# Mirror images and weight forms laid out in denser blocks in HBM

## The chip, the cores and the metric

The kernel runs on one NeuronCore of a Trainium2 chip. The metric is device time in microseconds (us) of one execution of the whole program; three executions of the kernel before took 1409.75, 1408.47 and 1409.6 us, with a median of 1409.6 us. Engines are called by the names that the profile uses: PE is TensorE (matmuls), DVE is VectorE, ACT is ScalarE, POOL is GpSimd, SP is SyncE, which here only issues DMAs.

## The reference

An attention with squared ReLU in place of softmax is followed by two MLPs without residuals, all in float32:

```python
def _attn_ref(u, v, z):            # u, v: 2 x 3008 x 256, z: 2 x 3008 x 64
    scores = (1.0 / S) * np.matmul(z, z.transpose(0, 2, 1))
    attn = np.maximum(scores, 0.0) ** 2
    return u * np.matmul(attn, v)

def reference(...):                # x: 6016 x 256, w_in: 256 x 2048, w_out: 2048 x 256
    x = _attn_ref(u, v, z).reshape(B * S, D)
    r = np.maximum(x @ moe_w_in, 0.0)
    x = (s * (r * r) + b) @ moe_w_out
    h = x @ moe2_w_in
    return (h * (1.0 / (1.0 + np.exp(-1.702 * h)))) @ moe2_w_out
```

The scores are symmetric: z serves as query and as key.

## The kernel before, in words

**Tiling.** The 3008 tokens of each batch are cut into chunks of 512 and a last one of 448 (NCH = 6). Attention goes chunk by chunk of queries (c); for each it runs over the keys in blocks of 128 (kc is the key chunk, t the block of 128 in it). Each float32 operand is split into a rounded part hi, which ACT makes by a cast, and a rest lo, which DVE makes by a subtraction, and the product of a block with v takes six matmuls (L484, L485, L489: v's hi and lo with hi, v's hi with lo), into two accumulators in PSUM, accA and accB by turns.

**Fresh and mirrored blocks.** Because of the symmetry a block of scores between two different chunks is computed once (class Fresh: matmuls L545, ReLU L549, square L552, cast hi L556, lo L560). DVE also transposes it, four blocks of 128 into one wide tile T (L585, 128 x 2048), and `park` writes T to an HBM tile H on GpSimd's DMA queue (L600), 1 MB. When the mirror image is wanted, with the chunks in the other roles, `fetch` reads it back as a wide tile R by four DMAs of 32 partitions each on SP's queue (L613), one for each quarter (x) of the image, and class Turned casts hi (L635) and takes lo (L639) from it. In names the order is bb, kc, c: the blocks with keys of chunk 4 and queries of chunk 2 of batch 0 are gathered in T_0_4_2, parked as H_0_4_2, and fetched as R_0_4_2 when chunk 4 holds the queries and chunk 2 the keys. There are 30 images in the whole run.

**Weights.** During attention the two layers' weights are loaded (wr, L670 and L674), converted on the engines, summed into the forms that the layers' products want, and written to HBM on GpSimd's queue: up_forms (L785, L789), down_whole (L794, quarters of the down weights) and down_forms (L800, L806, five arrays: a11 and s1 to s4). The layers read them again for every pair of chunks: `load_up` (L815, into a wide tile), `load_down` (L828, into a cell) and `load_forms`, which loads one or two of the eight blocks i of one form into one cell: two neighbours in one joined DMA (L842), others by one DMA each (L845).

**Layers.** Chunks go in pairs, in the order PAIRS = (4, 0, 1, 2, 3, 5). A product of 2 x 2 blocks is done with seven products in place of eight for the blocks i that SEVEN lists: all but i = 3 in layer 0 (`0, 1, 2, 4, 5, 6` of 0 to 7, so 3 and 7 are left out), and 0 to 6 in layer 1. Up-projection matmuls are L1088, down-projection ones L1256 and L1281.

**What sets the order.** Nothing is scheduled at run time. The program writes a list of operations, each with what it reads and writes, the engine, and a reckoned cost, and `ordered` lays them out in time for all engines at once; each engine then executes its instructions in that fixed order, each queue its DMAs. A move of kb KB is reckoned by `moves` as a time on a shared DMA pipe (`slow` is the factor that the diff changes):

```python
pipe = 1.05 * slow * kb * 1024 / run * (0.0085 + run / 27200) / 16
```

Tiles come from pools with fixed numbers of buffers (56 cells, 13 big, 5 wide, 4 PSUM tiles, 2 each of accA and accB), and an operation that needs a new tile is held back in the list while no buffer is free. R, T and the up weights share the five wide tiles. Other loads on SP's queue in the attention stage are ur (u, L909, four DMAs into a big tile; DVE transposes it at L927), vr (v, L444), zr (z, L366), and the rows f of the layers (L896).

Of the kernel before, what the change touches and what calls it, by code (L numbers as in the profile page):

```python
# [7 lines left out]
F32 = mybir.dt.float32  # L8
# [220 lines left out]
def attention_mlp_mlp_kernel(  # L229
# [13 lines left out]
    nc = tc.nc  # L243
# [3 lines left out]
    P = 128  # L247
    CH = 512
# [11 lines left out]
    NQ = NF // 2  # L260
# [9 lines left out]
    wide = ctx.enter_context(tc.tile_pool(name="wide", bufs=COUNTS["wide"]))  # L270
    const = ctx.enter_context(tc.tile_pool(name="const", bufs=1))
    hbm = ctx.enter_context(tc.tile_pool(name="hbm", bufs=1, space=bass.MemoryType.DRAM))
# [34 lines left out]
    ops, T = [], {}  # L307
# [10 lines left out]
    STORES = "POOL"  # L318
    to_hbm = dict(SP=nc.sync, POOL=nc.gpsimd)[STORES]

    def moves(kb, fs, reads=(), writes=(), new=(), engine="SP", run=2048, count=None, slow=1.0, **more):
        def f():
            for g in fs:
                g()

        count = count or len(fs)
        pipe = 1.05 * slow * kb * 1024 / run * (0.0085 + run / 27200) / 16
        put(engine, (0.7 if engine == "POOL" else 0.45) * count, 2.0, f, reads, writes, new, pipe=pipe, count=count, **more)

    def move(kb, f, *args, **more):  # L330
        moves(kb, [f], *args, **more)
# [263 lines left out]
    def park(bb, kc, c):  # L595
        key, H = ("T", bb, kc, c), ("H", bb, kc, c)

        def f():
            T[H] = hbm.tile([P, 4 * CH], F32, tag=f"H_{bb}_{kc}_{c}", name=f"H_{bb}_{kc}_{c}")
            to_hbm.dma_start(out=T[H], in_=T[key].rearrange("p b s r -> p (b s r)"))  # L600

        move(1024, f, [key], [H], engine=STORES, soon=0.5)

    def fetch(bb, kc, c):
        H, key = ("H", bb, kc, c), ("R", bb, kc, c)
        fs = []
        for x in range(4):

            def f(x=x):
                if key not in T:  # L610
                    T[key] = wide_tile(f"R_{bb}_{kc}_{c}").rearrange("p (g q) -> p g q", g=4)
                src = T[H].rearrange("(g p) (b q) -> b p g q", g=4, b=4)[x]
                nc.sync.dma_start(out=T[key][32 * x : 32 * x + 32], in_=src)  # L613

            fs.append(f)
        moves(1024, fs, [H], [key], [(key, "wide")], slow=1.55)

    class Turned:
        def __init__(self, session, bb, t, kc, c):
# [26 lines left out]


    up_forms = {(l, i): hbm.tile([P, 14 * P], F32, tag=f"uf{l}{i}", name=f"uf{l}{i}") for l in range(2) for i in range(NQ)}
    down_whole = {(l, i): hbm.tile([P, 2, CH], F32, tag=f"dw{l}{i}", name=f"dw{l}{i}") for l in range(2) for i in range(NQ)}
    down_forms = {  # L650
        (l, f): hbm.tile([P, NQ, 2 * P], F32, tag=f"df{l}{f}", name=f"df{l}{f}")
        for l in range(2)
        for f in ("a11", "s1", "s2", "s3", "s4")
    }
# [73 lines left out]
    def prepare(layer, i, with_sums):  # L728
# [49 lines left out]
            move(kb, lambda: f(T[key].bitcast(F32)), [key], [write], engine=STORES, **more)  # L778

        def part(f):  # L780
            return down_forms[layer, f][:, i].rearrange("p (h n) -> p h n", h=2)

        ws = sums_of(0, *[lambda o=o, k=k: up(o, k) for o in range(2) for k in range(2)])
        key = split(0, [(slice(0, CH), lambda: T[ws])], [ws])
# [7 lines left out]
        key = split(2, [(slice(0, CH), lambda: T[wf][:, :, 2 * P :])], [wf])  # L792
        for o in range(1 if i in always[layer] else 2):
            store(256, key, ("dw", layer, i, o), lambda to, o=o: to_hbm.dma_start(  # L794
                out=down_whole[layer, i][:, o].rearrange("p (h n) -> p h n", h=2),
                in_=to[:, :, 2 * P * o : 2 * P * o + 2 * P],
            ))
        if not with_sums:
# [24 lines left out]
    def load_down(layer, p, i, o):  # L823
        key = "down", layer, p, i, o

        def f():
            t = cell(f"d_{layer}_{p}_{i}_{o}", F32R)
            nc.sync.dma_start(out=t.bitcast(F32), in_=down_whole[layer, i][:, o])  # L828
            T[key] = t.rearrange("p (h n) -> p h n", h=2)

        move(256, f, [("dw", layer, i, o)], [key], [(key, "cell")])
# [2 lines left out]

    def load_forms(layer, p, f, some):
        key = "down", layer, p, f, some
        joined = len(some) == 2 and some[1] == some[0] + 1

        def run():
            t = cell(f"d_{layer}_{p}_{f}_{some[0]}", F32R).rearrange("p (q n) -> p q n", q=2)  # L840
            if joined:
                nc.sync.dma_start(out=t.bitcast(F32), in_=down_forms[layer, f][:, some[0] : some[0] + 2])  # L842
            for y, i in enumerate(some):
                if not joined:
                    nc.sync.dma_start(out=t[:, y].bitcast(F32), in_=down_forms[layer, f][:, i])  # L845
                T[key, i] = t[:, y].rearrange("p (h n) -> p h n", h=2)

        count = 1 if joined else len(some)
        moves(
            128 * len(some), [run], [("df", layer, f, i) for i in some], [key], [(key, "cell")], run=1024, count=count  # L850
        )
        for i in some:
            form_key[layer, p, i, f] = key
# [650 lines left out]
    def write_list():  # L1504
# [59 lines left out]
        for layer in range(2):  # L1564
            for p in PAIRS:
# [10 lines left out]
                for i, quad in enumerate(pair.quads):  # L1576
# [4 lines left out]
                        load_forms(layer, p, "s4", (i,))  # L1581
                    if some and i == NQ - 1:
                        for f in ("a11", "s1", "s2", "s3"):
                            for x in range(0, len(some), 2):
                                load_forms(layer, p, f, some[x : x + 2])
                        for x, names in enumerate(tail_of(pair)):
                            fixed.setdefault(k + 4 + x, []).extend(names)
                    if (layer, p, i) == (0, PAIRS[0], 4):
# [70 lines left out]
```

## Time and profile before

| | |
|---|---|
| time, median of 3 | 1409.6 us |
| the profiled execution: its time | 1408.94 us |
| its span | 1407.2 us |
| PE busy | 1387.8 us (99%), 6147 matmuls |
| PE weight loads (PEld) busy | 1148.5 us (82%) |
| DVE busy | 1310.3 us (93%), 2324 instructions |
| ACT busy | 1190.0 us (85%), 2308 instructions |
| POOL busy | 148.6 us (11%), 235 instructions |
| DMA | 322.61 MB, 229 GB/s in the mean |
| mean granted clock of PE | 0.997 |

The span runs from the first to the last recorded instruction; the execution takes 1.7 us more. Busy shares are means over the whole run, and weight loads run beside matmuls. Attention fills about the first 440 us, the layers the rest. In the rows shown further down, a releaser in brackets, as in [4.19 <-DMA R<-H], says that the engine sat idle for 4.19 us before this instruction and that a DMA into R from H ended the wait; SPq is the DMA queue that SyncE feeds. In lists of operations several equal ones in a row stand as one row with a count.

### The profile page before, as it was taken

The page shows a single profiled execution, that of the slowest core. Times are in us where ns is not written, and L with a number is a line of the kernel's source. Part 1 is how long each engine was busy: PE and PEld are TensorE (multiplying, and loading weights), DVE is VectorE, ACT ScalarE, POOL GpSimd, SP SyncE. Part 2 cuts the span into 40 slices and gives each one's busy share as a digit, 9 for nine tenths or more (in the row PEclk, how much of TensorE's full clock was granted, in tenths as well). Part 3 has the DMA queues.
Part 4 walks back from the last instruction along what each step waited for, and adds up shares of the span by engine and source line. Part 5 has one row for each costly group of instructions (what it writes and reads, how often), then busy time and mean ns, then how long its engine had stood idle before and what let it go on. Part 6 is the DMA issues. An engine that isn't in the chain of part 4 may idle for free.

```text
span 1407.2 us, 20260 instructions
## 1 busy us (share of the span) xinstructions
PE 1387.8 (99%) x6147; PEld 1148.5 (82%) x6147; DVE 1310.3 (93%) x2324; ACT 1190.0 (85%) x2308; POOL 148.6 (11%) x235
## 2 busy tenths in 40 slices
PE   8999999999999999999999999999999999999998
PEld 5888779888888888787888888888888788888897
DVE  7999886999998699999999999999989999999987
ACT  8999675999877598998989899998878796978685
POOL 3022210002211000001010101100010101010010
PEclk9999999999999999999999999999999999999999
DMA  7899898869999556677768576866757575666553
GB/s 171 245 296 282 250 276 197 239 211 269 274 246 342 187 198 210 254 239 266 258 214 270 200 260 215 291 222 212 252 175 268 160 267 161 230 199 198 181 183 105
DMA packets 194829, 322.61 MB, mean 229 GB/s; under 512 B 85408, under 2 KB 117728, under 8 KB 190880
## 3 DMA queue, kind: packets, MB, share of 16 engines
q1 hardware_dynamic: 172976, 241.69, 57.4%
q0 software_dynamic: 19008, 78.90, 15.6%
q10 hardware_dynamic: 2736, 0.74, 0.3%
q8 instruction: 48, 0.79, 0.2%
q14 instruction: 61, 0.50, 0.1%
HBM read 244.19 MB, written 77.07 MB: 228 GB/s over the span
## 4 chain that ended last, share of the span: by engine, by line
PE 81%; issue 6%; DVE 4%; DMA 3%; ACT 3%; SPq 2%; ACTq 0%; POOL 0%; DVEq 0%; POOLq 0%
PE ps_b L1088 8%; PE ps_d L1088 8%; PE ps_c L1088 8%; PE accB L1281 6%; PE ps_s L545 5%; PE accA L485 4%; PE accA L484 4%; PE ps_d L1281 4%; PE accA L489 4%; PE ps_a L1088 4%; PE accB L484 4%; PE accB L485 4%; PE accB L489 4%; PE ps_b L1281 4%; PE accA L1281 3%
## 5 line engine op out<-in xcount | busy, mean ns | idle before, releaser
L1211 DVE TENSOR_TENSOR lo<-g_c,hi 128x512 fp32r<-128x512 f32 (+1 forms) x540 | 345.3, 672 | 6.4 <-ACT hi L1207 5.4
L1207 ACT CAST hi<-g_c 128x512 fp32r<-128x512 f32 (+1 forms) x540 | 310.9, 616 | 9.7 <-DVE g_c L1196 6.8
L1088 PE MATMUL ps_d<-op_t,up 128*128 128x512 f32 (+1 forms) x432 | 121.6, 390 | 2.0 <-DVE g_c L1162 1.7
L1088 PE MATMUL ps_b<-op_t,up 128*128 128x512 f32 (+1 forms) x432 | 121.3, 389 | 1.0 <-ACT s_u L1137 0.9
L549 ACT ACTIVATE a<-ps_s 128x512 f32<-128x512 f32 (+1 forms) x168 | 103.2, 621 | 21.4 <-PE ps_s L545 21.4
L484 PE MATMUL accA<-hi,v 128*128 128x512 f32 x288 | 112.7, 391 | 2.0 <-ACT hi L556 2.0
L1174 ACT ACTIVATE g_c<-g_c 128x512 f32<-128x512 f32 (+1 forms) x144 | 89.5, 622 | 29.2 <-DVE g_c L1162 28.7
L485 PE MATMUL accA<-hi,v 128*128 128x512 f32 x288 | 113.0, 392 | 0.0
L560 DVE TENSOR_TENSOR lo<-a,hi 128x512 fp32r<-128x512 f32 (+1 forms) x156 | 103.8, 668 | 9.7 <-ACT hi L556 8.6
L552 ACT ACTIVATE a<-a 128x512 f32<-128x512 f32 (+1 forms) x168 | 110.6, 665 | 0.9
L484 PE MATMUL accB<-hi,v 128*128 128x512 f32 (+1 forms) x288 | 110.0, 382 | 0.8 <-DVE hi L566 0.8
L485 PE MATMUL accB<-hi,v 128*128 128x512 f32 (+1 forms) x288 | 109.8, 381 | 0.0
L556 ACT CAST hi<-a 128x512 fp32r<-128x512 f32 (+1 forms) x168 | 108.2, 649 | 0.7
L1196 DVE TENSOR_TENSOR g_c<-g_c,g_c 128x512 f32<-128x512 f32 (+1 forms) x156 | 105.0, 673 | 1.4
L545 PE MATMUL ps_s<-zq,zk 128*128 128x512 f32 (+1 forms) x336 | 101.6, 390 | 2.8 <-DVE zk L394 2.2
L1088 PEld LDWEIGHTS ps_d<-op_t,up 128*128 128x128 f32 x432 | 79.5, 188 | 21.7 <-DVE g_c L1162 5.3
L1088 PEld LDWEIGHTS ps_b<-op_t,up 128*128 128x128 f32 x432 | 79.7, 188 | 19.9 <-DVE g_c L1162 2.8
L1281 PE MATMUL accB<-hi,d 128*128 128x512 f32 (+1 forms) x312 | 95.0, 386 | 0.0
L585 DVE STREAM_TRANSPOSE T<-a 128x512 f32<-128x512 f32 x120 | 83.9, 700 | 7.9 <-DMA H<-T 4.7
L1177 ACT ACTIVATE g_c<-g_c 128x512 f32<-128x512 f32 (+1 forms) x144 | 88.2, 629 | 0.6
L639 DVE TENSOR_TENSOR lo<-R,hi 128x512 fp32r<-128x512 f32 x120 | 79.4, 678 | 7.9 <-ACT hi L635 3.6
L489 PE MATMUL accA<-lo,v 128*128 128x512 f32 x276 | 85.8, 392 | 0.3 <-DVE lo L560 0.3
(181 smaller groups left out, 3418.9 us busy)
## 6 DMA issues: line engine op xcount, KB each, us to landing
up<-uf SPq DMA_DIRECT2D x96, 896.0 KB
H<-T POOLq DMA_DIRECT2D x30, 1024.0 KB, 7.5
R<-H SPq DMA_DIRECT2D x120, 256.0 KB
d<-dw SPq DMA_DIRECT2D x114, 256.0 KB
d_s<-df1s SPq DMA_DIRECT2D x54, 256.0 KB
d_s<-df0s SPq DMA_DIRECT2D x72, 128.0 KB
f<-rows SPq DMA_DIRECT2D x18, 512.0 KB
d_s<-df0s SPq DMA_DIRECT2D x36, 256.0 KB
```

What stands on the lines that cost most here:

```text
L484: nc.tensor.matmul(T[k][:, :n], w[:, 0, cols], T[hi][:, :n], **start_flags(k, fresh))
L485: nc.tensor.matmul(T[k][:, :n], w[:, 1, cols], T[hi][:, :n], **start_flags(k, ()))
L489: nc.tensor.matmul(T[k][:, :n], w[:, 0, cols], T[lo][:, :n], **start_flags(k, ()))
L545: nc.tensor.matmul(T[self.p][:, :n], k, T[zq][:, h, :n], start=h == 0, stop=h == 1)
L552: nc.scalar.activation(out=T[self.a][:, :n], in_=T[self.a][:, :n], func=AF.Square)
L556: nc.scalar.copy(out=T[self.hi][:, :n], in_=T[self.a][:, :n])
L560: nc.vector.tensor_tensor(out=T[self.lo][:, :n], in0=T[self.a][:, :n], in1=T[self.hi][:, :n], op=ALU.subtract)
L1088: nc.tensor.matmul(to[:, :n], a[h], y[:, g, :n], start=first and j == 0, stop=False, skip_group_check=True)
L1196: nc.vector.tensor_tensor(out=self.get(to), in0=self.get(x), in1=self.get(y), op=ALU.subtract)
L1207: nc.scalar.copy(out=T[keys[0]][:, :n], in_=self.get(c))
L1211: nc.vector.tensor_tensor(out=T[keys[1]][:, :n], in0=self.get(c), in1=T[keys[0]][:, :n], op=ALU.subtract)
L1281: nc.tensor.matmul(to[:, :n], w[:, h, cols], g[:, :n], start=first and j == 0, stop=False, skip_group_check=True)
```

## The change

Three things change, and the order that follows from them.

First, an image lies in HBM as four quarters, H being [4, 128, 512] in place of [128, 2048]. The store still writes all four quarters of 128 partitions, now in pieces of 512 floats; a fetch of quarter x reads one contiguous block of 256 KB. The list reckons the store with a factor of 1.1 (1.0 before) and the fetches with 1.2 (1.55 before).

Second, down_whole is [2, 128, 512] in place of [128, 2, 512], and down_forms is [4, 128, 2, 256] in place of [128, 8, 256], two neighbouring blocks in one dense array.

Third, a joined load of two forms is now only possible for an even and the next odd block. In layer 0 the six blocks 0, 1, 2, 4, 5, 6 are therefore grouped as (0, 1), (2, 6), (4, 5), where they were (0, 1), (2, 4), (5, 6).

```diff
     def park(bb, kc, c):
...
-            T[H] = hbm.tile([P, 4 * CH], F32, tag=f"H_{bb}_{kc}_{c}", name=f"H_{bb}_{kc}_{c}")
-            to_hbm.dma_start(out=T[H], in_=T[key].rearrange("p b s r -> p (b s r)"))
-        move(1024, f, [key], [H], engine=STORES, soon=0.5)
+            T[H] = hbm.tile([4, P, CH], F32, tag=f"H_{bb}_{kc}_{c}", name=f"H_{bb}_{kc}_{c}")
+            to_hbm.dma_start(out=T[H].rearrange("b p q -> p b q"), in_=T[key].rearrange("p b s r -> p b (s r)"))
+        move(1024, f, [key], [H], engine=STORES, soon=0.5, slow=1.1)
...
     def fetch(bb, kc, c):
...
-                src = T[H].rearrange("(g p) (b q) -> b p g q", g=4, b=4)[x]
+                src = T[H][x].rearrange("(g p) q -> p g q", g=4)
                 nc.sync.dma_start(out=T[key][32 * x : 32 * x + 32], in_=src)
...
-        moves(1024, fs, [H], [key], [(key, "wide")], slow=1.55)
+        moves(1024, fs, [H], [key], [(key, "wide")], slow=1.2)
...
-    down_whole = {(l, i): hbm.tile([P, 2, CH], F32, tag=f"dw{l}{i}", name=f"dw{l}{i}") for l in range(2) for i in range(NQ)}
+    down_whole = {(l, i): hbm.tile([2, P, CH], F32, tag=f"dw{l}{i}", name=f"dw{l}{i}") for l in range(2) for i in range(NQ)}
...
-        (l, f): hbm.tile([P, NQ, 2 * P], F32, tag=f"df{l}{f}", name=f"df{l}{f}")
+        (l, f): hbm.tile([NQ // 2, P, 2, 2 * P], F32, tag=f"df{l}{f}", name=f"df{l}{f}")
...
-        joined = len(some) == 2 and some[1] == some[0] + 1
+        joined = len(some) == 2 and some[1] == some[0] + 1 and some[0] % 2 == 0
...
-                            for x in range(0, len(some), 2):
-                                load_forms(layer, p, f, some[x : x + 2])
+                            both = [(x, x + 1) for x in range(0, NQ, 2) if x in some and x + 1 in some]
+                            odd = [x for x in some if (x - x % 2, x - x % 2 + 1) not in both]
+                            for group in sorted(both + [tuple(odd[x : x + 2]) for x in range(0, len(odd), 2)]):
+                                load_forms(layer, p, f, group)
```

The accesses to down_whole and down_forms in `prepare`, `load_down` and `load_forms` follow the new shapes.

The order of DMAs on SP's queue, in the attention stage around the fetches of the images R_0_4_2 and R_0_4_3; before:

```order
L670 DMA wr_0_9_2045<-in_moe_w_in_dram 128x1x256 x2
L674 DMA wr_0_9_2045<-in_moe_w_out_dram 128x512
L909 DMA ur_3_2058<-in_u_dram 32x16x64 x4
L613 DMA R_0_4_2_2092<-H_0_4_2_1538 32x4x512 x4
L613 DMA R_0_4_3_2151<-H_0_4_3_1832 32x4x512 x4
L613 DMA R_0_5_0_2200<-H_0_5_0_786 32x4x512 x4
L909 DMA ur_4_2255<-in_u_dram 32x16x64 x4
L444 DMA vr_1_1_2297<-in_v_dram 32x4x256 x4
L613 DMA R_0_5_1_2400<-H_0_5_1_1218 32x4x512 x4
L613 DMA R_0_5_2_2462<-H_0_5_2_1623 32x4x512 x4
L613 DMA R_0_5_3_2515<-H_0_5_3_1982 32x4x512 x4
```

And after the change:

```order
L670 DMA wr_0_9_1989<-in_moe_w_in_dram 128x1x256 x2
L674 DMA wr_0_9_1989<-in_moe_w_out_dram 128x512
L613 DMA R_0_4_2_2051<-H_0_4_2_1548 32x4x512 x4
L613 DMA R_0_4_3_2076<-H_0_4_3_1832 32x4x512 x4
L909 DMA ur_3_2125<-in_u_dram 32x16x64 x4
L909 DMA ur_4_2165<-in_u_dram 32x16x64 x4
L613 DMA R_0_5_0_2202<-H_0_5_0_786 32x4x512 x4
L444 DMA vr_1_1_2267<-in_v_dram 32x4x256 x4
L670 DMA wr_0_10_2292<-in_moe_w_in_dram 128x1x256 x2
L674 DMA wr_0_10_2292<-in_moe_w_out_dram 128x512
L613 DMA R_0_5_1_2324<-H_0_5_1_1247 32x4x512 x4
L444 DMA vr_1_2_2416<-in_v_dram 32x4x256 x4
```

Both fetches move ahead of the load ur_3, ur_4 ahead of R_0_5_0, and the weight load wr_0_10 and the v load vr_1_2 ahead of R_0_5_1 and R_0_5_2.

The order on ScalarE at the first casts of R_0_4_2 (L549, L552 and L556 belong to the chunk's own fresh blocks, L763 to the weights that are prepared on the side); before:

```order
L635 CAST hi_2211<-R_0_4_1_1925 128x512
L549 ACTIVATE a_2214<-ps_s_2195 128x512
L552 ACTIVATE a_2214<-a_2214 128x512
L556 CAST hi_2223<-a_2214 128x512
L635 CAST hi_2234<-R_0_4_2_2092 128x512
L549 ACTIVATE a_2236<-ps_s_2218 128x512
L635 CAST hi_2240<-R_0_4_2_2092 128x512
L552 ACTIVATE a_2236<-a_2236 128x512
L549 ACTIVATE a_2260<-ps_s_2242 128x512
L556 CAST hi_2266<-a_2236 128x512
```

And after the change:

```order
L635 CAST hi_2217<-R_0_4_1_1911 128x512
L549 ACTIVATE a_2219<-ps_s_2207 128x512
L552 ACTIVATE a_2219<-a_2219 128x512
L556 CAST hi_2228<-a_2219 128x512
L635 CAST hi_2239<-R_0_4_2_2051 128x512
L549 ACTIVATE a_2243<-ps_s_2225 128x512
L763 CAST forms_0_4_1_2248<-wf_0_8_2170 128x256
L552 ACTIVATE a_2243<-a_2243 128x512
L763 CAST forms_0_4_2_2261<-wf_0_8_2170 128x512
L556 CAST hi_2272<-a_2243 128x512
L549 ACTIVATE a_2275<-ps_s_2250 128x512
L763 CAST forms_0_4_1_2248<-wf_0_8_2170 128x128
```

The first cast of R_0_4_2 keeps its place between the fresh blocks' operations; its second cast comes later, and the casts of a weight form have moved in before it.

## Rows read from the trace of the kernel before

**Rows 1.** Part 1 of the page: each engine's busy us, share, instructions.
```profile
PE 1387.8 (99%) x6147; PEld 1148.5 (82%) x6147; DVE 1310.3 (93%) x2324; ACT 1190.0 (85%) x2308; POOL 148.6 (11%) x235
```

**Rows 2.** Chain that ended last, 995 to 1010 us: start, us, what.
```profile
995.97 4.08 PE ps_b L1281 x18
```

**Rows 3.** Busy by 20 us: PE, PEld, DVE, ACT, POOL; clock, DMA, GB/s.
```profile
140.00:160.00 20.00, 18.77 (x82) 14.64 (x81) 15.23 (x28) 12.34 (x24) 4.09 (x6) 1.00 0.91 243
...
180.00:200.00 20.00, 17.97 (x72) 14.27 (x72) 16.62 (x36) 12.02 (x24) 3.24 (x5) 0.91 1.10 282
300.00:320.00 20.00, 20.00 (x90) 16.58 (x89) 19.77 (x39) 18.07 (x36) 1.07 (x2) 1.00 0.71 218
560.00:580.00 20.00, 18.71 (x80) 14.34 (x79) 19.67 (x34) 18.88 (x37) 5.26 (x8) 1.00 0.88 314
640.00:660.00 20.00, 18.21 (x78) 14.19 (x77) 18.07 (x31) 17.39 (x34) 3.44 (x5) 1.00 0.87 295
```

**Rows 4.** Chain that ended last, 130 to 200 us.
```profile
172.67 1.94 SPq L613
...
176.19 7.75 DMA R<-H
...
188.60 0.85 PE accA L489 x2
```

**Rows 5.** Timelines of ACT and PE: start, us, work, idle time before it.
```profile
184.03 0.62 ACT L635 CAST hi<-R 128x512 fp32r<-128x512 f32 x1 [4.19 <-DMA R<-H]
...
187.23 0.50 PE L484 MATMUL accA<-hi,v 128*128 128x512 f32 x1 [2.03 <-ACT hi L556]
```

**Rows 6.** Timeline of SP's queue, 100 to 200 us.
```profile
129.35 2.59 SPq L909 DMA_DIRECT2D ur<-in_u_dram  x4
...
160.58 11.99 SPq L909 DMA_DIRECT2D ur<-in_u_dram  x4
```

**Rows 7.** By 1 us from 412: us, granted clock, DMA share, GB/s.
```profile
413.00:414.00 1.00, 1.00 1.02 221
414.00:415.00 1.00, 1.00 1.08 231
```

**Rows 8.** The same by 0.5 us from 1079, and SP's timeline before it.
```profile
1079.00:1079.50 0.50, 1.00 1.11 420
1079.50:1080.00 0.50, 1.00 1.03 395
...
1075.52 1.91 SPq L842 DMA_DIRECT2D d_s<-df1s  x3
```

**Rows 9.** SP's timeline from 176 us, and 1 us of all engines.
```profile
214.69 3.67 SPq L444 DMA_DIRECT2D vr<-in_v_dram  x4
...
220.00:221.00 1.00, 1.00 (x6) 0.93 (x6) 0.68 (x2) 0.55 (x2) 0.00 (x0) 1.00 1.09 225
```

**Rows 10.** Timeline of DVE, 140 to 200 us.
```profile
160.64 0.68 DVE L639 TENSOR_TENSOR lo<-R,hi 128x512 fp32r<-128x512 f32 x1
...
199.34 0.70 DVE L927 STREAM_TRANSPOSE ut<-ur 128x512 f32<-128x512 f32 x1
```

**Rows 11.** DMA issues (count, KB, us to landing), and the image tile's landings.
```profile
out_dram<-o POOLq DMA_DIRECT2D x40, 128.0 KB, 3.0
...
DMA to landing us min/median/max: 4.2/7.5/10.9
```

**Rows 12.** DVE's and POOL's timelines, and SP's waits (us, times, longest).
```profile
152.23 0.71 DVE L585 STREAM_TRANSPOSE T<-a 128x512 f32<-128x512 f32 x1 [4.70 <-DMA H<-T]
...
141.61 0.57 POOL L600 DMA_DIRECT2D H<-T  x1 [4.77 <-DVE T L585]
...
SPq L613 <- DMA H<-T: 91.4, 10, 16.8
```

**Rows 13.** ACT's and PE's timelines at the next chunk.
```profile
221.60 0.57 ACT L556 CAST hi<-a 128x448 fp32r<-128x448 f32 x1
...
216.16 0.36 PE L484 MATMUL accB<-hi,v 128*128 128x448 f32 x1
```

More of the change, by code (lines that the diff above doesn't have):

```diff
@@ L780, in part @@
         def part(f):
-            return down_forms[layer, f][:, i].rearrange("p (h n) -> p h n", h=2)
+            return down_forms[layer, f][i // 2, :, i % 2].rearrange("p (h n) -> p h n", h=2)
         ws = sums_of(0, *[lambda o=o, k=k: up(o, k) for o in range(2) for k in range(2)])
@@ L794, in prepare @@
             store(256, key, ("dw", layer, i, o), lambda to, o=o: to_hbm.dma_start(
-                out=down_whole[layer, i][:, o].rearrange("p (h n) -> p h n", h=2),
+                out=down_whole[layer, i][o].rearrange("p (h n) -> p h n", h=2),
                 in_=to[:, :, 2 * P * o : 2 * P * o + 2 * P],
@@ L827, in f @@
             t = cell(f"d_{layer}_{p}_{i}_{o}", F32R)
-            nc.sync.dma_start(out=t.bitcast(F32), in_=down_whole[layer, i][:, o])
+            nc.sync.dma_start(out=t.bitcast(F32), in_=down_whole[layer, i][o])
             T[key] = t.rearrange("p (h n) -> p h n", h=2)
@@ L841, in run @@
             if joined:
-                nc.sync.dma_start(out=t.bitcast(F32), in_=down_forms[layer, f][:, some[0] : some[0] + 2])
+                nc.sync.dma_start(out=t.bitcast(F32), in_=down_forms[layer, f][some[0] // 2])
             for y, i in enumerate(some):
                 if not joined:
-                    nc.sync.dma_start(out=t[:, y].bitcast(F32), in_=down_forms[layer, f][:, i])
+                    nc.sync.dma_start(out=t[:, y].bitcast(F32), in_=down_forms[layer, f][i // 2, :, i % 2])
                 T[key, i] = t[:, y].rearrange("p (h n) -> p h n", h=2)
```

## The prediction

> **What bounds the kernel now.** I read first the page's busy table, then the busy time by stretches of 20 us, then the chain that ended last around the two worst stretches, and last the timelines of the engines that it names. The table has TensorE busy for 1387.8 us of the 1407.2 us span [rows 1], so everything outside it is 19.4 us. A busy matmul can still be a slow one, so I counted matmuls. Eighteen 512-column matmuls in a row take 4.08 us [rows 2], 226.7 ns each; 20 us hold 88.2 of them. The undisturbed stretch at 300 us shows 90 (those across an edge count in both neighbours), the one at 140 us 82, the one at 180 us 72, at a granted clock of 0.91, and two in the later layers 80 and 78 [rows 3]. In time that is 1.4, 3.7, 1.9 and 2.3 us lost. So TensorE is the bound and only such gaps can be won: about 5 us in the attention stage, the rest in the layers behind it, beside the start and the end, which the change doesn't touch.
>
> The gap at 180 us has its cause in the chain: the next image fetch is issued only at 172.67, it is still in flight at 176.19, for 7.75 us more, and the chain ends in two matmuls that take 0.85 us [rows 4], where two at full speed take 0.45. [...] What stood ahead of that fetch on the SP queue was the line that loads u, L909: its four loads took 11.99 us from 160.58, beside large stores; the same four took 2.59 us at 129 us [rows 6].
>
> **The fetches themselves.** The list now reckons an image fetch 1.2/1.55 = 0.77 times as long as before. Does it get shorter? With almost nothing but image fetches running, the DMA engines are full (a share of 1.02 and 1.08) at 221 to 231 GB/s [rows 7]. One fetch moves 2 KB pieces that lie 8 KB apart in HBM into 32 partitions. The joined weight-form loads of L842 move 2 KB pieces, also 8 KB apart, into 128 partitions: three of them were issued from 1075.52, and adding up the bytes of the queue puts them into the stretch from about 1079.1 to 1081, which ran at 395 to 420 GB/s [rows 8]. The other way round, the v loads of 214.69, whose source is a dense block but whose target is 32 partitions, end the plateau at 220 us, at 225 GB/s [rows 9]. So the rate goes with the partitions written, not with the gaps in the source, and the change leaves the 32 partitions as they are. I take the fetch as unchanged, 1.05 MB at 223 GB/s = 4.7 us for the four pieces of an image; the other end is 400 GB/s, 2.6 us.
>
> [...]
>
> The weight forms (down_whole, down_forms) get denser too. Their loads already run at 395 to 420 GB/s from pieces 8 KB apart, so I cost them at 0. The regrouping in layer 0, (0,1), (2,6), (4,5) for (0,1), (2,4), (5,6), issues the same four DMAs.
>
> **What moves.** Since a fetch is reckoned shorter, the list sets the SP queue anew. The image R_0_4_2, the one that was late, and R_0_4_3 now go ahead of the u load ur_3, not behind it. ur_3 costs nothing there: the transposes that read it began at 199.34 us [rows 10], 27 us after its issue ended. R_0_4_2 needs a free wide tile; R_0_3_1 was read for the last time at 160.64 + 0.68 = 161.3 [rows 10], by counting L639's reads back from those of the late image. So it can be issued at 161.3 instead of 172.67, 11.3 us earlier. Even if it takes as long as before, from 172.67 to 176.19 + 7.75 = 183.9, thus 11.3 us, it lands at 172.6; ScalarE comes to it at 184.03 - 4.19 = 179.8. The wait goes with 7 us to spare, and the lost 3.7 us with it: **-3.7 us**. What is late next there is work of the same engines that ran without waits.
>
> **The stores.** A store now writes 512 pieces of 2 KB instead of 128 of 8 KB; no such store is in the trace. Nearest rows: the output stores, 512 pieces in 128 KB, land after 3.0 us; the image stores after 4.2 at best, 7.5 median [rows 11]. Taking off the data at 400 GB/s (0.3 and 2.6 us) leaves 2.7 against 1.6 us: at most 1.1 us more per store. Who waits: VectorE's transposes at 152.23 waited 4.70 us for the store issued at 141.61, whose landing frees their tile [rows 12], and TensorE lost the 1.4 us of that stretch. A later landing costs there one for one. [...] Between -1.4 and +1.1 I take **+0.6**, nearer to the row of 512 pieces. On GpSimd itself nothing waits but more stores.
>
> **The layers behind.** Of 6165 TensorE instructions some 570 change places, line and buffer numbers set aside, most of them in layer 0 (from the next weights' decoding, the regrouping, and the order of row loads). Losses there are gaps of 1 to 2 us like those at 560 and 640 us, behind ScalarE or VectorE, none behind a DMA. I cost the shuffle at 0, between -3 and +3, the size of one and a half such gaps.
>
> Sum: -3.7 + 0.6 = -3.1 us. The profiled execution took 1408.94 us, 1.7 us above its span; the median of 1409.6 is 0.7 higher, and I carry the difference over: 1409.6 - 3.1 = **1406.5 us**, mostly faster by more than the 0.2% (2.8 us) that a measurement of this kernel can tell from no change.
>
> **Rivals.** First, given back at the next chunk: behind ur_4 the new queue puts the loads wr_0_10 and vr_1_2 ahead of R_0_5_1 and R_0_5_2. At 400 and 223 GB/s they take 1.3 and 2.35 us, so R_0_5_3 could come 3.7 us later. Its casts stand on ScalarE ahead of the chunk's own block, whose cast ended at 222.2; TensorE, which began this chunk at 216.16 [rows 13], needs it 48 matmuls of 448 columns (198 ns) later, at 225.7. Spare is 3.5 us, and TensorE now comes 3.7 us earlier: the gain would go again, 1409.5 to 1410. Against it: the queue has won back about 9 us from the slow u load, so these fetches should come earlier, not later. 20%.
>
> Second, the list is right and the fetches do run at up to 400 GB/s. Then the shortened queue also takes most of the remaining 1.7 us of this stage, and images leave room for the stores: about 1404. Rows 7 to 9 speak against it. 10%.
>
> Third, slower: the 2 KB stores land much later. Place: the tile that the transposes at 152 us wait for, and the fetches that follow a store at once (SP waited for a store's landing ten times, 91.4 us [rows 12]). If landings grow by g, TensorE loses g at 152 us and about g at two fetches without spare; 3g - 3.7 passes +2.8 us from g = 2.2 us on. At g = 3 the time is 1409.6 - 3.7 + 9 = 1415. For it: that one store already took 10.6 us to land. Against: the piece count bounds it at 1.1 us. 14%.
>
> Fourth, layer 0's new order loses two more gaps like that at 640 us and a further one like that at 560: +6.5, with the rest about 1413. 8%.
>
> **How the numbers follow.** The forecast has 48%; its own range, from the bounds (-3.7 - 1.4 - 3 and -3.7 + 1.1 + 3), is 1401.5 to 1410. It gives 40 points of faster and 8 of no change; the second rival adds 10 of faster, the first 16 of no change and 4 of slower, the third 14 of slower, the fourth 3 and 5. That is 50% faster, 27% within 0.2%, 23% slower. For 8 in 10 the range runs from 1401.5 to 1412.5; it leaves out the third rival's far end and part of the fourth.
>
> **What would show it.** In the trace of the changed kernel: plateaus of fetches still near 223 GB/s (at 400 the second rival holds); ScalarE's cast of R_0_4_2 without a wait and the matmul count of that stretch near 88 at a granted clock of 1.00; no new ScalarE wait on R_0_5_3 that ends in a TensorE gap near 225 us; image stores landing at 7.5 to 8.6 us in the median, and the transposes' wait of 4.7 us neither gone nor over 6. The prediction is wrong if R_0_4_2 finds no free tile, if TensorE stalls at the next chunk, or if layer 0 loses more than it did.

## The result and the profile after

The changed kernel takes 1420.26 us in the median of five runs (1419.11 to 1422.71), the kernel before 1409.28 us in five; the ratio is 1.0085, with a 95% interval of 1.007 to 1.010. The forecast was 3 us faster; it is 11 us slower, above the range. The profiled execution took 1420.26 us, its span is 1418.5 us. The page's table, against [rows 1]:

```profile
PE 1393.1 (98%) x6147; PEld 1151.1 (81%) x6147; DVE 1313.0 (93%) x2324; ACT 1189.7 (84%) x2308; POOL 154.3 (11%) x235
```

TensorE is busy for 5.3 us more with the same matmuls, and outside its busy time lie 25.4 us, not 19.4. The busy time by stretches of the changed kernel, to be held against [rows 3]:

```profile
140.00:160.00 20.00, 18.07 (x73) 13.95 (x72) 14.07 (x26) 12.75 (x24) 3.74 (x5) 0.91 0.94 259
180.00:200.00 20.00, 19.86 (x88) 16.10 (x87) 19.94 (x41) 15.20 (x30) 5.31 (x8) 1.00 0.97 278
200.00:220.00 20.00, 15.71 (x57) 12.13 (x56) 12.35 (x22) 9.93 (x20) 1.58 (x3) 0.83 0.99 266
220.00:240.00 20.00, 18.86 (x92) 16.94 (x92) 11.80 (x21) 12.61 (x26) 0.00 (x0) 1.00 0.86 188
480.00:500.00 20.00, 17.62 (x74) 14.63 (x73) 12.21 (x26) 11.47 (x22) 0.67 (x1) 0.91 0.31 109
640.00:660.00 20.00, 20.00 (x88) 16.00 (x87) 19.87 (x36) 15.53 (x29) 1.80 (x3) 1.00 0.54 190
```

The stretch at 180 us has its 88 matmuls, as forecast. But the one at 200 us has 57, at a granted clock of 0.83, and at 480 us, early in layer 0, 74 are left. In the kernel before the same two stretches were full:

```profile
200.00:220.00 20.00, 20.00 (x92) 16.93 (x91) 14.12 (x25) 13.52 (x26) 3.45 (x5) 1.00 1.06 269
480.00:500.00 20.00, 20.00 (x90) 16.62 (x89) 19.29 (x33) 19.08 (x36) 0.68 (x1) 1.00 0.50 184
```

So that stretches of all runs can be compared, here is the time that TensorE loses in each: its length less 226.7 ns for each matmul of 512 columns in it and 198 ns for each of 448, an estimate from the same time per column (from 229.95 us of the kernel before 28 of them in a row took 5.67 us, 202.5 ns each); a matmul across an edge counts in each stretch by its part. Single values are good to about a microsecond, and an undisturbed 200 to 300 us shows 0.7.

| lost, us | 0 to 200 | 200 to 300 | 300 to 470 | 470 to 500 | rest |
|---|---|---|---|---|---|
| before | 15.4 | 0.7 | 1.2 | 0.2 | 25.1 |
| changed | 13.7 | 11.2 | 1.7 | 4.6 | 22.7 |

The layers behind even win 2.4 us and the first 200 us 1.7; the loss, 10.5 and 4.4 us more than before, stands at two places. How the first comes about is seen on SP's queue. Its timeline after the change (start, us, line, what, count), against [rows 9]:

```profile
187.50 1.80 SPq L444 DMA_DIRECT2D vr<-in_v_dram  x4
189.51 1.51 SPq L670 DMA_DIRECT2D wr<-in_moe_w_in_dram  x2
191.81 0.35 SPq L674 DMA_DIRECT2D wr<-in_moe_w_out_dram  x1
192.83 4.80 SPq L613 DMA_DIRECT2D R<-H  x4
197.73 8.85 SPq L444 DMA_DIRECT2D vr<-in_v_dram  x4
207.17 11.16 SPq L613 DMA_DIRECT2D R<-H  x12
```

R_0_5_1 is issued at 192.83, R_0_5_2 only at 207.17 (199.29 in the kernel before); between them stands vr_1_2, which took 8.85 us to issue. The chain that ended last, there and at the matmuls that follow:

```profile
189.51 11.45 DMA wr<-in_moe_w_in_dram
200.96 0.02 issue
200.98 5.39 DMA vr<-in_v_dram
...
207.17 3.93 DMA R<-H
...
214.43 0.85 PE accA L489 x2
```

The weight load wr_0_10 of 189.51 was 11.45 us in flight. A load of vr_1_2 that stands eight places behind it was issued 0.02 us after it had landed. The cast of R_0_5_2 then kept ScalarE waiting, and the operation behind it TensorE, in the timelines of ACT, DVE and PE:

```profile
211.16 0.62 ACT L635 CAST hi<-R 128x512 fp32r<-128x512 f32 x1 [6.36 <-DMA R<-H]
...
206.38 0.43 DVE L685 TENSOR_SCALAR pw<-wr 128x512 uint32<-128x512 uint32 x1 [3.18 <-DMA vr<-in_v_dram]
...
212.35 0.79 PE L484 MATMUL accA<-hi,v 128*128 128x512 f32 x1 [3.22 <-ACT hi L556]
```

While the wr load was in flight the DMA engines were full (a share of 1.04 to 1.06), with an image store and four stores of prepared weights, issued from 189.29 to 193.33, among others. By 2 us (granted clock, DMA share, GB/s):

```profile
188.00:190.00 2.00, 1.00 1.06 235
196.00:198.00 2.00, 1.00 1.04 414
200.00:202.00 2.00, 1.00 1.06 386
```

The second place is a store that lands late. The chain at the start of layer 0, and the matmul behind it in PE's timeline:

```profile
475.65 5.96 DMA df1s<-forms
...
481.75 0.62 ACT op_b L989
...
482.91 0.97 PE L1088 MATMUL ps_a<-op_b,up 128*128 128x512 f32 x3 [2.38 <-ACT ps_a L1154]
```

A store of layer 1's weight forms, 5.96 us from issue to landing, holds up a cast of op_b, an early operand of layer 0, and TensorE waits 2.38 us behind it; in the kernel before GpSimd issued no store between 431 and 482 us.

### The profile page after: what moved, and what is told of

Same layout as the page of the kernel before. It is cut to its first block, busy times and chain, and to the rows that moved or that the text cites. A ratio compares the mean times of both kernels' runs of the same rounds, so it can differ in the third digit from the quotient of the medians.

```text
span 1418.5 us, 20194 instructions
## 1 busy us (share of the span) xinstructions
PE 1393.1 (98%) x6147; PEld 1151.1 (81%) x6147; DVE 1313.0 (93%) x2324; ACT 1189.7 (84%) x2308; POOL 154.3 (11%) x235
## 4 chain that ended last, share of the span: by engine, by line
PE 74%; DVE 8%; DMA 7%; ACT 5%; issue 3%; SPq 1%; POOL 0%; ACTq 0%; DVEq 0%; POOLq 0%
PE ps_b L1088 8%; PE ps_c L1088 8%; PE ps_d L1088 7%; PE accB L1281 7%; PE ps_d L1281 5%; PE ps_b L1281 4%; PE ps_a L1088 4%; PE ps_s L545 4%; PE accA L1281 3%; PE accA L485 3%; PE accA L484 3%; PE accA L489 3%; PE ps_c L1281 3%; PE accA L1256 3%; PE accB L484 3%
## 5 line engine op out<-in xcount | busy, mean ns | idle before, releaser
L1207 ACT CAST hi<-g_c 128x512 fp32r<-128x512 f32 (+1 forms) x540 | 310.0, 616 | 12.1 <-DVE g_c L1196 8.6
L549 ACT ACTIVATE a<-ps_s 128x512 f32<-128x512 f32 (+1 forms) x168 | 102.5, 614 | 19.9 <-PE ps_s L545 19.9
L552 ACT ACTIVATE a<-a 128x512 f32<-128x512 f32 (+1 forms) x168 | 109.9, 658 | 1.0
L556 ACT CAST hi<-a 128x512 fp32r<-128x512 f32 (+1 forms) x168 | 107.5, 642 | 1.7 <-issue 1.1
```

The lines of the kernel that those rows point to most:

```text
L552: nc.scalar.activation(out=T[self.a][:, :n], in_=T[self.a][:, :n], func=AF.Square)
L556: nc.scalar.copy(out=T[self.hi][:, :n], in_=T[self.a][:, :n])
L1207: nc.scalar.copy(out=T[keys[0]][:, :n], in_=self.get(c))
```

## Experiments: list, images or weights

Theory A was that the new order costs the time, because 1.2 tells the list of a fetch that doesn't exist; B, that the 2 KB stores cost it; C, the weight layouts and the regrouping. Three kernels take the parts one by one. e1_list_only is the kernel before with the factors alone:

```diff
-        move(1024, f, [key], [H], engine=STORES, soon=0.5)
+        move(1024, f, [key], [H], engine=STORES, soon=0.5, slow=1.1)
...
-        moves(1024, fs, [H], [key], [(key, "wide")], slow=1.55)
+        moves(1024, fs, [H], [key], [(key, "wide")], slow=1.2)
```

> Only the two factors of the list are changed (fetch 1.2, store 1.1); images, weight forms and grouping stay as before. Theory A, the new order costs the time (the queue is set as if fetches were shorter, which they are not): 1417 to 1421 us, with the TensorE gap of about 5 us at 207 to 217 us and the one of about 4.7 us at 480 us. Theory B, the 2 KB stores cost it: 1408 to 1410 us, or less by the 3 us of the gap at 185 us. Theory C, the regrouping and the weight layouts: the same as B.

1425.31 us, 1.0122 (1.0104 to 1.0139) times the kernel before, above the range of theory A. Every engine's order is that of the changed kernel, and the same two places lose: 14.0 us at 200 to 300, 5.8 at 470 to 500. All of the loss is in the two numbers; it is even 5 us larger than in the changed kernel.

e2_images_only is the kernel before with the new H alone, without the factors:

```diff
-            T[H] = hbm.tile([P, 4 * CH], F32, tag=f"H_{bb}_{kc}_{c}", name=f"H_{bb}_{kc}_{c}")
-            to_hbm.dma_start(out=T[H], in_=T[key].rearrange("p b s r -> p (b s r)"))
+            T[H] = hbm.tile([4, P, CH], F32, tag=f"H_{bb}_{kc}_{c}", name=f"H_{bb}_{kc}_{c}")
+            to_hbm.dma_start(out=T[H].rearrange("b p q -> p b q"), in_=T[key].rearrange("p b s r -> p b (s r)"))
...
-                src = T[H].rearrange("(g p) (b q) -> b p g q", g=4, b=4)[x]
+                src = T[H][x].rearrange("(g p) q -> p g q", g=4)
```

> Only the layout of the image tile in HBM is changed, with the factors of before, so every engine keeps the order of before. Theory A: 1408 to 1411 us, store landings a little longer (8 us in the median), fetch plateaus still at 220 to 230 GB/s. Theory B: 1413 to 1420 us. If the fetches were really quicker from dense quarters: plateaus above 300 GB/s and 1404 to 1407 us.

1407.51 us, 0.9994 (0.9983 to 1.0005). The order is that of before on every engine, the stores land after 8.2 us in the median, and the time is the same: B falls.

e3_weights_only is the changed kernel with these lines and those of e1 as they were before:

```diff
-            T[H] = hbm.tile([4, P, CH], F32, tag=f"H_{bb}_{kc}_{c}", name=f"H_{bb}_{kc}_{c}")
+            T[H] = hbm.tile([P, 4 * CH], F32, tag=f"H_{bb}_{kc}_{c}", name=f"H_{bb}_{kc}_{c}")
...
-        moves(1024, fs, [H], [key], [(key, "wide")], slow=1.2)
+        moves(1024, fs, [H], [key], [(key, "wide")], slow=1.55)
```

> Only the layouts of the weight forms and the regrouping in layer 0 are changed; images and factors as before, so that the attention stage keeps its order. Theory C: the loss of some 11 us stands here. Theories A and B: 1407 to 1411 us, with nothing moved before 440 us.

1408.42 us, 0.9997 (0.9988 to 1.0007): C falls too. e17_layouts_only, run last, has all layouts and the regrouping, and the factors of before:

```diff
-        move(1024, f, [key], [H], engine=STORES, soon=0.5, slow=1.1)
+        move(1024, f, [key], [H], engine=STORES, soon=0.5, slow=1.0)
...
-        moves(1024, fs, [H], [key], [(key, "wide")], slow=1.2)
+        moves(1024, fs, [H], [key], [(key, "wide")], slow=1.55)
```

> The changed kernel with the two factors of before (fetch 1.55, store 1.0): all layouts and the regrouping stay. If layouts and order add up as e2 and e3 did alone: 1406 to 1410 us. If they cost something together: over 1411 us.

1403.80 us, 0.9969 (0.9957 to 0.9981), faster than either expectation. Without the two numbers the change gains 4.6 us. Between e1 and the changed kernel, which have one order, the layouts gave 5 us as well. Why they give more together than e2 and e3 apart isn't settled; e17 has the order of e3 on every engine, so the list plays no part in it; in the profile of e17 the late cast of [rows 5] no longer waits.

## Experiments: what the fetch is bound by

e4_wide_fetch is the kernel before with the four DMAs cut the other way, each into all 128 partitions:

```diff
-                src = T[H].rearrange("(g p) (b q) -> b p g q", g=4, b=4)[x]
-                nc.sync.dma_start(out=T[key][32 * x : 32 * x + 32], in_=src)
+                src = T[H].rearrange("(g p) (b q) -> g b p q", g=4, b=4)[x]
+                nc.sync.dma_start(out=T[key][:, x], in_=src)
```

> Everything as before, order included, but the four DMAs of a fetch are cut the other way: each writes 512 columns of all 128 partitions in place of 2048 columns of 32. Theory of partitions (the fetch rate goes with the partitions written): plateaus of fetches at 380 to 420 GB/s and a time of 1403 to 1408 us. If the gaps in the source or the 2 KB pieces set the rate: plateaus stay at 220 to 230 GB/s and the time within 1408 to 1411 us.

1559.88 us, 1.1075 (1.1058 to 1.1091), neither expectation. With little but fetches running, e4 moves, by 1 us:

```profile
161.00:162.00 1.00, 1.00 0.27 98
163.00:164.00 1.00, 0.50 0.26 102
```

A quarter of the DMA engines' share of before, 0.26 to 0.27 for the 1.02 to 1.08 of [rows 7], and half the rate, 98 to 102 GB/s for 221 to 231. The source's outermost dimension had become 4 (it was 32); that this sets the share was my reading.

e7_rows_fetch keeps the 128 partitions and gives the source 128 rows, by another H; the store becomes four DMAs, the factors are 1.55 and 1.0:

```diff
-            T[H] = hbm.tile([4, P, CH], F32, tag=f"H_{bb}_{kc}_{c}", name=f"H_{bb}_{kc}_{c}")
-            to_hbm.dma_start(out=T[H].rearrange("b p q -> p b q"), in_=T[key].rearrange("p b s r -> p b (s r)"))
+            T[H] = hbm.tile([P, 4 * CH], F32, tag=f"H_{bb}_{kc}_{c}", name=f"H_{bb}_{kc}_{c}")
+            rows_of = T[H].rearrange("(b j) (g q) -> g j b q", b=4, g=4)
+            for g in range(4):
+                to_hbm.dma_start(out=rows_of[g], in_=T[key][32 * g : 32 * g + 32].rearrange("p b s r -> p b (s r)"))
...
-                src = T[H][x].rearrange("(g p) q -> p g q", g=4)
-                nc.sync.dma_start(out=T[key][32 * x : 32 * x + 32], in_=src)
+                src = T[H][:, CH * x : CH * x + CH]
+                nc.sync.dma_start(out=T[key][:, x], in_=src)
```

> The image lies in HBM as the fetch wants it, one 8 KB row for each partition of R; each of the four DMAs of a fetch writes 512 columns of all 128 partitions from 128 rows, and the store is cut into four DMAs of 32 partitions. Factors of before (1.55, 1.0), weights as in the changed kernel. The fourfold outer dimension of e4, which left a quarter of the DMA engines' share in use, is gone. Theory of partitions: plateaus at 380 to 420 GB/s and 1402 to 1408 us, or up to 1411 if the narrower stores land 2 to 3 us later. If 2 KB pieces set the rate: 220 to 230 GB/s.

1401.21 us, 0.9950 (0.9935 to 0.9964), the fastest of all, 2.6 us under e17, though the two intervals overlap. Each quarter of its image stores lands after 5.6 us in the median, and the transposes at 152 us of [rows 12] don't wait. e11_rows_095 has the same fetches reckoned at 0.95:

```diff
-        moves(1024, fs, [H], [key], [(key, "wide")], slow=1.55)
+        moves(1024, fs, [H], [key], [(key, "wide")], slow=0.95)
```

> e7 (fetches into all 128 partitions), now with a fetch reckoned at 0.95, which is 2.7 us in the list and what 1.05 MB take at 400 GB/s. Theory A1 (a price that is true gives a good order): 1397 to 1403 us. Rival: a short price pulls weight loads and stores together whatever the fetch does, as in the changed kernel: 1408 to 1420 us, with losses at 150 us and at 200 to 220 us.

1419.14 us, 1.0079 (1.0063 to 1.0095). At 210 us it shows two stretches of fetches, and a later one of v loads into 32 partitions:

```profile
210.00:212.00 2.00, 1.00 1.05 393
212.00:214.00 2.00, 1.00 1.03 382
...
216.00:218.00 2.00, 1.00 1.12 220
```

With 128 rows in the source the share of the 128-partition fetch is 1.03 to 1.05, not 0.27. So the rate goes with the partitions written, 382 to 393 against 220 GB/s. And yet a price that is true for the fetch lost as much as 1.2 had: theory A, as I had put it, falls. Ahead of the next batch's first z load its queue had wr_0_10, which the kernel before issues at 248.38 behind all of them, and from vr_1_2 on nineteen loads of v, of which the kernel before has four there. It lost 7.7 us at 200 to 300 us, nearly all behind 220, and 5.7 at 300 to 470. By its time the rival holds, though not by the places it named; that these loads cost it is not shown by an edit of its own.

## Experiments: the price as a dial

Three kernels are the changed one with another factor for the fetch and the store left at 1.1; e5:

```diff
-        moves(1024, fs, [H], [key], [(key, "wide")], slow=1.2)
+        moves(1024, fs, [H], [key], [(key, "wide")], slow=1.67)
```

e6_fetch_14 has 1.4 in this line, e15_fetch_19 has 1.9. At 1.67 the list reckons 4.7 us for an image, what 1.05 MB take at 223 GB/s.

> The changed kernel with one number other: a fetch reckoned at 1.67, which makes it 4.7 us in the list, what it takes in the trace (1.05 MB at 223 GB/s). Theory A1 (the time is lost because 1.2 prices the fetch too low): 1404 to 1411 us. Theory A2 (the list's order is sensitive, the factor of before happened to give a good order, any other draw costs several us): 1412 to 1425 us, with gaps at other places.

> The changed kernel with the fetch reckoned at 1.4, halfway back. A1: between the two, 1408 to 1415 us, the eleventh weight load (wr_0_10) still early or late, and the gap at 205 to 217 us there only if it is early. A2: anywhere from 1405 to 1425 us, not ordered by the factor.

> The changed kernel with the fetch reckoned at 1.9, 5.4 us in the list, more than it takes. If the true price is the best one: 1404 to 1412 us, worse than e5 (1402.9). If a dearer fetch only keeps unneeded loads away: 1400 to 1404 us, as good as e5 or better.

| factor | list's us per image | time, us | against before | lost 0 to 200 | 200 to 300 | 300 to 470 | 470 to 500 | rest |
|---|---|---|---|---|---|---|---|---|
| 1.2 (changed) | 3.4 | 1420.26 | 1.0085 (1.0070 to 1.0100) | 13.7 | 11.2 | 1.7 | 4.6 | 22.7 |
| 1.4 (e6) | 3.9 | 1412.97 | 1.0027 (1.0015 to 1.0038) | 13.3 | 0.7 | 3.5 | 0.3 | 28.9 |
| 1.55 (e17) | 4.4 | 1403.80 | 0.9969 (0.9957 to 0.9981) | 12.7 | 0.7 | 0.6 | 0.5 | 22.9 |
| 1.67 (e5) | 4.7 | 1402.85 | 0.9959 (0.9944 to 0.9974) | 11.3 | 0.7 | 1.3 | 0.5 | 23.8 |
| 1.9 (e15) | 5.3 | 1407.84 | 0.9990 (0.9981 to 0.9999) | 9.2 | 0.7 | 5.2 | 0.5 | 26.0 |

(e17 has the store at 1.0.) The best factor lies about where the price is true, though e5 and e17 can't be told apart and e5 is a little faster than A1 allowed; e6 fits both theories. But each draw has its gaps at other places, and only at 1.2 are the two large ones there. Two more runs show that a factor isn't good by itself: e10_old_layout_167 is the kernel before with 1.67,

```diff
-        moves(1024, fs, [H], [key], [(key, "wide")], slow=1.55)
+        moves(1024, fs, [H], [key], [(key, "wide")], slow=1.67)
```

> The kernel before with one number other: a fetch reckoned at 1.67 in place of 1.55; no layout is changed. If the price alone carries the gain of e5: 1402 to 1405 us. If the denser layouts have a part in it: 1406 to 1410 us.

1405.83 us, 0.9981 (0.9971 to 0.9992), between the two expectations, and e12_rows_167 is e7 with the same line and the store at 1.1:

```diff
-        move(1024, f, [key], [H], engine=STORES, soon=0.5, slow=1.0)
+        move(1024, f, [key], [H], engine=STORES, soon=0.5, slow=1.1)
```

> e7's fetches with the fetch reckoned at 1.67 and the store at 1.1, the order of e5. If the gains of e5 (5.8 us) and e7 (7.4 us) come from different gaps: 1394 to 1399 us. If both take away the same gaps at 150 and 185 us: 1399 to 1403 us.

1405.21 us, 0.9981 (0.9972 to 0.9990), above both ranges and slower than either of the two that it joins (against e5 the intervals just touch). It loses only 9.0 us by 200 us, but 4.7 at 300 to 470, where a cast of an image waits 9.93 us for its fetch.

e14_others_dearer keeps the price of the fetch and makes all other moves dearer by a third:

```diff
-        pipe = 1.05 * slow * kb * 1024 / run * (0.0085 + run / 27200) / 16
+        pipe = 1.4 * slow * kb * 1024 / run * (0.0085 + run / 27200) / 16
...
-        moves(1024, fs, [H], [key], [(key, "wide")], slow=1.2)
+        moves(1024, fs, [H], [key], [(key, "wide")], slow=0.9)
```

> The changed kernel with the fetch reckoned as in it, but every other move dearer by a third (1.4 in place of 1.05 in the price of all moves, 0.9 in place of 1.2 for the fetch). If the old fetch price stood in for traffic that the list reckons too cheap: wr_0_10 goes back behind the z loads and the time is 1400 to 1411 us. If the price of the fetch itself decides: 1415 to 1425 us.

1415.76 us, 1.0043 (1.0026 to 1.0060), by its time the second case, by its queue the first: the loss at 200 to 300 us is down to 0.9 us, and wr_0_10 stands behind the z loads. So that stretch can be cured with the price of the fetch left as it is, by taking the stage's other traffic for dearer; the rest of that order is worse (5 us more than before lost by 110 us, 5.9 at 300 to 470).

## Experiments: which load does it

Four kernels are the changed one with a piece of its order put elsewhere after the list is made. e8_late_decode moves the conversion of wr_0_10 on VectorE and ScalarE, not the loads; weight(i), left out here, picks these operations:

```diff
...
+    at = max(x for x, i in enumerate(result) if ops[i].engine == "DVE" and ("R", 0, 5, 2) in ops[i].keys) + 1
+    early, late = result[:at], result[at:]
+    result = [i for i in early if not weight(i)] + [i for i in early if weight(i)] + late
```

> The changed kernel, but the operations on VectorE and ScalarE that convert the weights of wr_0_10 stand behind the last use of R_0_5_2; the loads keep their places on the queues. If VectorE, held for 3.2 us by these late weights, is what keeps the tile for R_0_5_2 from coming free: its fetch is issued about 3 us earlier, TensorE's loss of 7.8 us at 200 to 220 us falls to 2 to 5 us, and the time to 1414 to 1417 us. If the full DMA engines alone keep the fetch late: the loss stays at 7 to 8 us and the time at 1419 to 1421 us.

1418.66 us, 1.0067 (1.0052 to 1.0082), between the two expectations; the loss at 200 to 220 us is 6.4 us, 7.4 in the changed kernel. R_0_5_2 was issued at 205.75, as soon as vr_1_2 was out: the wait of 3.18 us on VectorE had held it for 1.4 us, the queue for the rest.

Which of the two loads it is, e6 shows already. Its queue has vr_1_2 ahead of R_0_5_2 like the changed kernel, but not wr_0_10, which is issued only at 242.17; the DMA engines are as full:

```profile
190.00 3.59 SPq L613 DMA_DIRECT2D R<-H  x4
193.90 1.86 SPq L444 DMA_DIRECT2D vr<-in_v_dram  x4
198.52 13.89 SPq L613 DMA_DIRECT2D R<-H  x12
...
200.00:220.00 20.00, 20.00 (x93) 17.16 (x92) 12.63 (x21) 12.70 (x25) 2.30 (x4) 1.00 1.06 290
```

There vr_1_2 takes 1.86 us to issue, R_0_5_2 follows at 198.52, and TensorE loses nothing. The order of e6 differs at other places too, but by this pair it is the weight load that makes the fetch late, and the v load alone costs nothing.

e9_loads_behind moves wr_0_10 and vr_1_2 behind R_0_5_4. behind(order, which, engine, tile) puts the chosen operations behind the last one of that engine that touches the tile; weight stands for the conversion, loads for SP's loads of the tiles named (in the two runs further down, loads is given the tiles):

```diff
...
+    def loads(i):
+        return ops[i].engine == "SP" and {("wr", 0, 10), ("vr", 1, 2)} & set(ops[i].keys)
+
+    result = behind(result, weight, "DVE", ("R", 0, 5, 3))
+    result = behind(result, loads, "SP", ("R", 0, 5, 4))
```

> The changed kernel, but wr_0_10 and vr_1_2 stand behind R_0_5_4 on SP's queue, and the conversion of wr_0_10 behind the last use of R_0_5_3. All else as in the changed kernel. If these two loads ahead of the fetches are what makes them late: R_0_5_2 is issued before 202 us, not at 207.2, the loss of 7.8 us at 200 to 220 us falls under 2 us and the time to 1408 to 1413 us. If the DMA engines are full there whatever stands in the queue: R_0_5_2 lands as late as before and the time stays at 1416 to 1420 us.

1419.90 us, 1.0084 (1.0066 to 1.0102), by its time the second case. Its stretches say otherwise:

```profile
200.00:220.00 20.00, 20.00 (x92) 17.02 (x91) 13.29 (x22) 12.59 (x24) 2.38 (x4) 1.00 1.06 288
220.00:240.00 20.00, 12.42 (x53) 10.09 (x52) 10.00 (x18) 10.23 (x22) 0.00 (x0) 0.85 0.80 179
```

The loss at 200 us is gone (0.1 us), and as much stands 20 us later (12.1 us by 250), behind the z loads of the next batch, which wr_0_10 and twelve loads of v now precede. e13_z_first puts zr_1_1, zr_1_0 and zr_1_2 ahead of wr_0_10, vr_1_3, vr_1_4 and vr_1_5:

```diff
...
+    result = behind(result, weight, "DVE", ("zk", 1, 2))
+    result = behind(result, loads(("vr", 1, 2)), "SP", ("R", 0, 5, 4))
+    result = behind(result, loads(("wr", 0, 10), ("vr", 1, 3), ("vr", 1, 4), ("vr", 1, 5), (("vr", 1, 5), 1)), "SP", ("zr", 1, 2))
```

> The changed kernel with one stretch of SP's queue put back as in the kernel before: the fetches R_0_5_1 to R_0_5_4, vr_1_2 and the z loads zr_1_1, zr_1_0, zr_1_2 come ahead of wr_0_10, vr_1_3, vr_1_4 and vr_1_5; the conversion of wr_0_10 follows the use of these z loads. If the loads pulled ahead are the cause of the loss at 200 to 270 us (11.9 us in the changed kernel): it falls under 3 us, and the time to 1408 to 1413 us. If the DMA engines are full there in any order: the loss shows again 20 to 40 us later, 1416 to 1421 us.

1420.98 us, 1.0088 (1.0071 to 1.0105), and again the gap has wandered:

```profile
200.00:220.00 20.00, 20.00 (x92) 17.02 (x91) 13.33 (x22) 12.60 (x25) 2.41 (x4) 1.00 1.06 288
220.00:240.00 20.00, 20.00 (x101) 18.48 (x100) 12.95 (x22) 11.06 (x25) 0.55 (x1) 1.00 0.84 191
240.00:260.00 20.00, 13.74 (x53) 11.52 (x52) 12.95 (x26) 10.04 (x21) 0.00 (x0) 0.83 0.48 90
```

What stands behind now is zr_1_4, whose queue still has ur_10, wr_0_10 and wr_0_11 ahead of it. e16_all_z_first puts all z loads of the batch ahead of both weight loads, as in the kernel before, and the conversion of both behind the last z operand; behind goes here by the last operation that writes the tile:

```diff
...
+    result = behind(result, weight, "DVE", ("zk", 1, 5))
+    result = behind(result, loads(("vr", 1, 2)), "SP", ("R", 0, 5, 4))
+    result = behind(result, loads(("vr", 1, 3), ("vr", 1, 4), ("vr", 1, 5), (("vr", 1, 5), 1)), "SP", ("zr", 1, 2))
+    result = behind(result, loads(("ur", 10), ("wr", 0, 10), ("wr", 0, 11)), "SP", ("zr", 1, 5))
```

> The changed kernel with SP's queue from R_0_5_1 to zr_1_5 in the order of the kernel before: all fetches, v and z loads ahead of wr_0_10, ur_10 and wr_0_11, and the conversion of both weight blocks behind the last z operand. If the weight loads pulled ahead are the cause of the loss at 200 to 290 us (11.9 us in the changed kernel): it falls under 3 us and the time to 1408 to 1413 us, the loss of 4.7 us at 480 us staying. If the stretch has too much to move in any order: 1416 to 1422 us, with the loss behind yet another load.

1412.97 us, 1.0027 (1.0014 to 1.0040), the first case by its time: some 7 of the 11 us are back. By its loss at 200 to 300 us it is neither: 7.4 us for 11.2.

```profile
200.00:220.00 20.00, 20.00 (x93) 17.14 (x92) 12.30 (x20) 12.54 (x24) 1.38 (x3) 1.00 1.07 275
...
260.00:280.00 20.00, 18.01 (x67) 14.33 (x68) 19.87 (x42) 20.00 (x43) 2.27 (x3) 0.83 0.78 201
```

From 200 to 250 us TensorE loses 0.7 us, 9.4 in the changed kernel, with the DMA engines as full as in e9 (1.07 at 200 us, 1.06 there). What is left at 250 to 270 us, 6.7 us, is the edit's own: VectorE converts two weight blocks in one go there (255.09 to 261.5), and TensorE waits for the lo's behind them. The store ahead of op_b still costs 3.3 us at 470 to 500. So the cause of the first loss is shown: loads that nobody needs yet, pulled ahead of fetches and z loads in a queue whose engines are full (a share of 1.04 to 1.06 in the changed kernel). At the first gap it is wr_0_10; of the loads ahead of the z loads these runs don't say how much each costs. In the runs without this loss (e5, e6, e14, e15 and the kernel before) wr_0_10 is issued between 242 and 257 us, in the changed kernel, e1 and e11 before 192.

## Why the prediction was wrong, point by point

**The fetches themselves: right.** The changed kernel's fetches run as before; with little else, at 412 us:

```profile
412.00:413.00 1.00, 1.00 1.05 206
413.00:414.00 1.00, 1.00 1.17 245
```

That is 226 GB/s in the mean, beside the 221 to 231 of [rows 7]; e11 shows the partitions as the cause, with 382 to 393 GB/s into 128 of them and 220 into 32.

**R_0_4_2: right.** It is issued at 162.78, no cast of it waits, and the stretch at 180 to 200 us loses 0.5 us where it lost 3.9: -3.4 for the forecast -3.7. The waits of [rows 5] are gone, and so is the lower clock behind them, here in the kernel before by 2 us (granted clock, DMA share, GB/s):

```profile
188.00:190.00 2.00, 0.52 1.07 230
```

In the changed kernel the whole stretch has 1.00. The slow ur loads didn't go; eight of them take 11.65 us from 173.62.

**The stores: about right.** They land after 8.1 us in the median (7.5 before) and the transposes of [rows 12] wait 5.87 us for 4.70:

```profile
153.66 0.71 DVE L585 STREAM_TRANSPOSE T<-a 128x512 f32<-128x512 f32 x1 [5.87 <-DMA H<-T]
...
DMA to landing us min/median/max: 4.6/8.1/11.6
```

That is 1.2 us, at the bound of +1.1; with the lower clock behind it (0.91 at 140 to 160 us, 1.00 before) the stretch at 140 to 180 us loses 1.4 us more than before. That the 1.4 us go, the other end of the term, no run shows: the four u loads of 11.99 us [rows 6] took 11.36 us in e2, with 2 KB stores, 11.26 in e3, with stores as before, and 7.79 in e17, with 2 KB stores and the order of e3, where they were issued 4.1 us earlier.

**The next chunk: the step that failed.** The first rival named the place and the two loads, wr_0_10 and vr_1_2 ahead of R_0_5_1 and R_0_5_2, and priced them at 3.7 us, 512 KB each at 400 and 223 GB/s. That is the price on engines with little else to move [rows 7, 8]. R_0_5_2 was issued 14.3 us behind R_0_5_1, whose own issue took 4.8: 9.5 us lay between them. The engines were full (1.04 to 1.06), so what was put ahead delayed all behind it, and a load was issued 0.02 us after one eight places ahead had landed. wr_0_10, priced at 1.3 us, cost 7.4 us at 200 to 220 us; without it e6 lost nothing there. The rows ahead had shown both, a u load of 11.99 us [rows 6] and full engines [rows 7, 9]. And I stopped at R_0_5_3: the excerpt of the order was cut before the z loads, where the same loads cost as much when they stand there, as e9 and e13 show. The point against it, that the queue had won back 9 us, was no argument: the u loads had only moved, and R_0_5_0 was issued at 185.38, not at 179.65 as before. With 20% and at most 1410 us this rival should have been the forecast, at +10.

**The layers: inside the bound by luck.** +4.4 us at 470 to 500 stands behind a DMA, where I had written that none of the gaps stands, and by itself exceeds the bound of 3. The rest of the layers won 2.4 us, which I hadn't foreseen either; the two make +2.0.

The sum: forecast -3.7 + 0.6 + 0. The table gives -1.7 to 200 us, +10.5 at 200 to 300, +0.5 to 470, +4.4 to 500 and -2.4 behind it, +11.3 in all, the difference of the spans.

What stays open: why the layouts together give 4.6 us where e2 and e3 give none, and why at 1.2 layer 1's store falls just ahead of op_b; the latter wasn't tried by an edit of its own.

## What to carry to other kernels

A number in a planner's price list is a change of the whole order: time it by itself, with everything else unchanged, before it rides along with a layout; here the layouts gain 4.6 us, and the two numbers turn that into a loss of 11. Where a queue's engines are full, price a load that moves ahead by what waits behind it, to the end of the stretch, not by its own bytes at a free rate (wr_0_10: 1.3 us by its bytes, 7.4 lost). A gap that wanders when one load is moved says that too much stands ahead, not that the suspect was innocent: put the whole stretch back before giving up the cause.

## What the runs showed of the hardware that was not expected

The cut of a DMA decides more than its bytes: the same 1 MB ran at 98 to 102 GB/s with a source of outermost dimension 4, at 206 to 245 into 32 partitions and at 382 to 393 from 128 rows into 128 partitions. And the faster fetch is worth little here by itself: e7, with the fetches that ran at 1.7 times the rate in e11 and quicker stores, is 2.6 us faster than e17, with intervals that overlap.
